# Sums over partitions by way of DRAM instead of products with ones, in a fused state-space and mixture-of-experts kernel

## The chip, the cores and the metric

The kernel runs on one core of a Trainium2 chip. Its time is the device time of one execution in microseconds. Engines are named as the profile names them: PE is TensorE (PEld its weight loads), ACT is ScalarE, DVE is VectorE, POOL is GpSimd, SP is SyncE, which here only issues DMAs.

## The reference

One input sequence of 2048 tokens by 512 channels is normalised, and two layers read the result. Their outputs and the input are added.

```python
x = A_u
xn = _layernorm(x, axis=-1)
return x + _A_ref(xn, ...) + _B_ref(xn, B_w_gate, B_w1, B_w2)

# A: a long convolution of every channel with a generated filter
P = jnp.exp(logdA[:, :, None] * l[None, None, :])
K = jnp.einsum("dn,dnl,dn->dl", Cc, P, dB).real      # filter, 512 x 2048
y = irfft(rfft(pad(xn)) * rfft(pad(K)))[:L] + xn * Dskip

# B: 8 experts, all 8 chosen for every token (K = 8 = E), gates by softmax
for e in range(E):
    h = _silu(xf @ w1[e]) @ w2[e]                    # 512 -> 1792 -> 512
    out = out + w * h
```

All of it is in float32. The kernel gets there with float16 products: every operand is split into a high and a low float16 part, and three products are summed.

## The kernel before, in words

**The main loop.** Eight experts, each over four blocks of 512 tokens (`tb`), each in four steps of hidden columns (`d`, `DQS`: two pairs of columns for d = 0, 1, 2 and one pair for d = 3), each in four slots (`s`). In a slot PE runs one or two groups of the first product (`product`, L1307, into the PSUM tiles `hb`, seven groups for a `d`), then some units of the second product (`pop`, L1290 to L1292, into `y`). ACT copies `hb` on (L1526, L1534, `keep` L1521), applies the activation (L1323) and makes the high part `ahl` (L1327); DVE makes the low part (L1336). A slot of d = 3 has half as many first products as one of d = 0, 1, 2.

**Beside it.** The order on every engine is written out by hand: `slot` is called 510 times, and at its end it does, in this order, some weight steps (`work_on`) and some of the convolution (`bg_run`). Generators hand out the work; `clock` counts the cost given to PE, ACT and DVE; `clock["slot"]` is the number of the slot.

- *Weight steps.* For each next expert the weights are loaded twice. In the first pass ACT squares each piece and sums along the row (`square`, L438). `prepass_end` then adds the partial sums of a row on DVE (L406), adds over the 128 partitions (`pow2_total`), and DVE makes a power of two of the sum, with which ACT and DVE split the weights in the second pass (`w1_split`, `w2_split`, L442 and L445). It runs twice for each expert, once for `w1` and once for `w2`. Between its parts, which are steps of `piece_end`, at least two slots pass.
- *Convolution.* 32 chunks of 16 channels. For a chunk, PE generates the filter (`s4_kernel`, L729). `s4_kernel_out` squares it on ACT with a row sum into `krow` (L737) and copies it to `ksb` (L738). SP stores `ksb` to DRAM as `kd` (L743) and loads it back in another layout as `kt`, in four transfers (L745). `s4_ksplit` adds `krow` over the partitions (`pow2_total`), makes the scale (`s4_kscale`), and splits `kt` (L758 on ACT, L763 on DVE).

**The sum over partitions.** `pow2_total` multiplies the column by a 128 x 128 matrix of ones in float32 (L170), so that every partition gets the sum, in a PSUM bank, and ACT copies it out (L165). There is one such small bank (`ps_s`, tag `s4`), which the filter, the transforms and the transposes use as well: `take_bank` runs the pending read-out before the bank is used again, and `bank_free` says if it may be used in this slot, and runs a pending read-out.

Other names that the prediction needs: the token operand `xop` is reloaded from DRAM by SP in d = 3 (L1517); the partial products `scC` and `scB` are added to by POOL's DMAs (L1492) before ACT reads them.

Of the kernel before, what the change touches and what calls it, by code (L numbers as in the profile page):

```python
# [9 lines left out]
F32 = mybir.dt.float32  # L10
F16 = mybir.dt.float16
I32 = mybir.dt.int32
AF = mybir.ActivationFunctionType
# [4 lines left out]
P = 128  # L18
# [14 lines left out]
def s4_moe_kernel(  # L33
# [15 lines left out]
    nc = tc.nc  # L49
    V, S, T = nc.vector, nc.scalar, nc.tensor  # L50
# [17 lines left out]
    sb = ctx.enter_context(tc.tile_pool(name="sb", bufs=2))  # L68
# [3 lines left out]
    dr = ctx.enter_context(tc.tile_pool(name="dr", bufs=1, space=bass.MemoryType.DRAM))  # L72
# [24 lines left out]
    uts = {}  # L97

    clock = {"slot": 0, "pe": 0.0, "pe0": 0.0, "dve": 0.0, "dve0": 0.0, "left": 0.0,
             "act": 0.0, "act0": 0.0, "pe1": 0.0, "actleft": 0.0}  # L100
    bank = {"out": None, "at": -1}

    def take_bank(out=None):

        f, bank["out"] = bank["out"], None
        if f:
            f()
            bank["at"] = clock["slot"]
        bank["out"] = out

    def bank_free():

        if bank["out"]:
            take_bank()
        return clock["slot"] > bank["at"]

# [44 lines left out]
    def pow2_total(rows, n, nm, out=None):  # L161

        st = sb.tile([P, n], F32, tag="p2a", name=f"st_{nm}", bufs=2)
        def read():
            S.copy(st, tot[:, :n])  # L165
            if out:
                out()
        take_bank(read)
        tot = ps_s.tile([P, 512], F32, tag="s4", name=f"tot_{nm}")
        T.matmul(tot[:, :n], ones, rows, start=True, stop=True)  # L170
        return st

    def pow2_scale(dst, st, nm, add=0):

        it = sb.tile([P, st.shape[-1]], I32, tag="p2b", name=f"it_{nm}", bufs=2)
        V.tensor_scalar(it, st.bitcast(I32), 24, 23, op0=ALU.logical_shift_right, op1=ALU.logical_shift_left)
        V.tensor_scalar(dst.bitcast(I32), it, -1.0, float((204 + add) << 23), op0=ALU.mult, op1=ALU.add)

    def pow2_inverse(dst, src, add=0):

        V.tensor_scalar(dst.bitcast(I32), src.bitcast(I32), -1.0, float((254 + add) << 23), op0=ALU.mult, op1=ALU.add)
# [217 lines left out]
    def w1_scales(sc, st, nm):  # L399
        pow2_scale(sc[:, 0:1], st, nm, -1)  # L400
        pow2_inverse(sc[:, 2:3], sc[:, 0:1], -XSH)
        times(sc[:, 3:4], sc[:, 0:1], 1 - ASH)

    def prepass_end(e, w, n):
        r = sb.tile([P, 1], F32, tag="r2", name=f"r2_{e}_{w}")
        V.tensor_reduce(r, rows[e, w][:, :n], axis=AX.X, op=ALU.add)  # L406
        yield
        st = pow2_total(r, 1, f"w{e}_{w}")
        yield
        if bank["out"]:  # L410
            take_bank()
        if w == 0:
            sc = scales[e] = sb.tile([P, 5], F32, tag="sc", name=f"sc{e}", bufs=2)
            w1_scales(sc, st, f"w{e}")
        else:
            sc = scales[e]
            pow2_scale(sc[:, 1:2], st, f"v{e}")
            pow2_inverse(sc[:, 4:5], sc[:, 1:2])
            V.scalar_tensor_tensor(sc[:, 4:5], sc[:, 4:5], float(2.0 ** (XSH - 1 + ASH)), sc[:, 2:3], op0=ALU.mult, op1=ALU.mult)
            ge_ = sb.tile([P, NT], F32, tag="gse", name=f"gse{e}", bufs=2)  # L420
            gates_e[e] = ge_
            if e > 1:
                V.tensor_scalar(ge_, gate[:, :, e], sc[:, 4:5], None, op0=ALU.mult)
# [17 lines left out]
    def hilo(dst, raw, sc):  # L441
        S.activation(dst[:, 0], raw, AF.Copy, scale=sc)  # L442

        def low():
            V.scalar_tensor_tensor(dst[:, 1], raw, sc, dst[:, 0], op0=ALU.mult, op1=ALU.subtract)  # L445
            clock["dve"] += tt_(raw.free_size())
        return low
# [9 lines left out]

    def w1_split(e, pr, raw):

        dst = w1s[pr].rearrange("p a o c -> p a (o c)")  # L460
        return hilo(dst[:, :, 0:6 * P], raw[:, 0:3, :].rearrange("p o c -> p (o c)"), w1_scale(e, pr))

# [2 lines left out]
        return hilo(dst[:, :, 6 * P:14 * P], tw.rearrange("p o c -> p (o c)"), w1_scale(e, pr))  # L465

    def w2_split(e, pr, raw):
        return hilo(w2s[pr].rearrange("p a f d -> p a (f d)"), raw.rearrange("p a c -> p (a c)"), scales[e][:, 1:2])

    class Item:  # L470
# [6 lines left out]
    done = set()  # L477
# [19 lines left out]
        return it  # L497

    def piece_end(e, w, n, ready):
        st = {}  # L500

        def s0(raw):
            st["g"] = prepass_end(e, w, n)
            step(0)
            clock["dve"] += 0.2

        def step(n):
            st["at"] = now()
            next(st["g"], None)
            done.add((e, w, n))  # L510

        def s1(raw):
            step(1)

        def s2(raw):
            step(2)
            clock["dve"] += 2.5

        def later():
            return now() > st["at"] + 1 and bank_free() and now() + 1 not in turns  # L520
        its = [Item(None, [s0], ready), Item(None, [s1], later), Item(None, [s2], later)]
        for it in its:
            it.e, it.w = e, w
        return its

    def fetch():

# [22 lines left out]
        return True  # L550

    def work_on(limit):
        while limit > 0:
            fetch()
            it = None
            for n, c in enumerate(work[:6]):
                if c.load is None:
                    if n == 0 and can(c):
                        it = c
                        break  # L560
                    if n == 0 and (c.e, c.w, 0) in done:
                        continue
                    break
                if c.raw is not None and can(c):
                    it = c
                    break
            if it is None:
                break
            if it.sums and len(it.steps) == it.n:
                live["tw"], it.at = True, now()  # L570
            low = it.steps.pop(0)(it.raw)
            limit -= 1
            last = not it.steps
            if last:
                work.remove(it)
            if low:
                lows.append((low, last, it.sums and last, it.made))
            elif last and it.load is not None:
                live["n"] -= 1
        fetch()  # L580
# [16 lines left out]
    s4 = {}  # L597
# [136 lines left out]
    def s4_kernel_out(c):  # L734
        ksb = sb.tile([P, 4, 4, NI], F32, tag="ksb", name=f"ksb{c}", bufs=1)
        row = s4["krow", c] = sb.tile([P, 1], F32, tag="krow", name=f"krow{c}", bufs=2)
        S.activation(ksb.rearrange("p j g m -> p (j g m)"), s4["kgen"].rearrange("p g x -> p (g x)"), AF.Square, accum_out=row)  # L737
        S.copy(ksb, s4["kgen"].rearrange("p g (j m) -> p j g m", j=4))  # L738
        clock["act"] += 2 * at_(256)
        s4["ke", c] = now()  # L740
        kt = sb.tile([P, DC, NI], F32, tag="kt", name=f"kt{c}", bufs=1)
        kd = kds[c % 2]
        nc.sync.dma_start(kd, ksb.rearrange("p j g m -> p j (g m)"))  # L743
        for jh in range(4):
            nc.sync.dma_start(kt[32 * jh:32 * jh + 32].rearrange("x (s g) m -> x s (g m)", s=4),  # L745
                              kd[:, jh, :].rearrange("(s x) c -> x s c", s=4))
        s4["kt", c] = kt

    def s4_kscale(c):

# [121 lines left out]
    def at_(n):  # L872

        return n / 1050 + 0.17
# [10 lines left out]
    def now():  # L885
        return clock["slot"]
# [28 lines left out]
    def bank_wait():  # L915
        while not bank_free():
            yield None

    def until(*keys, more=1):

        for key in keys:
            while key not in s4 or now() <= s4[key] + more:
                yield None
# [41 lines left out]
    def s4_ksplit(c):  # L965

        yield from until(("ke", c))
        yield from bank_wait()
        s4["kst", c] = pow2_total(s4["krow", c], 1, f"k{c}", lambda: s4.update({("read", c): now()}))
        s4["total", c] = now()  # L970
        yield None
        while ("read", c) not in s4:
            bank_free()
            if ("read", c) not in s4:
                yield None
        yield from until(("read", c), more=0)
        s4_kscale(c)
        yield 0.6
        yield None
        if c:  # L980
            yield from until(("kf", c - 1), more=0)
        s4_khigh(c)
        yield None
        yield None
        s4_klow(c)
        s4["kl", c] = now()
        yield tt_(256)
# [73 lines left out]
    for pr in range(3, NPR):  # L1061
        for h in range(2):
            n = 2 * (pr - 3) + h
            tag, bufs = ("sE", 1) if n == 0 else ("sCB", 3) if n < 4 else ("stg", 4)
# [303 lines left out]
    turns = set()  # L1368
# [57 lines left out]
    for n, (g, a) in enumerate(halves):  # L1426
        s0 = 20 + 4 * n
# [61 lines left out]
    later = []  # L1489
# [173 lines left out]
```

## Time and profile before

| | |
|---|---|
| time, median of 3 runs (lowest, highest) | 2345.7 us (2345.11, 2345.76) |
| the profiled execution: its own time | 2344.99 us |
| the profiled execution: span of its instructions | 2343.2 us |
| granted PE clock | 1.0 |
| busy: PE, PEld, DVE, ACT, POOL | 2324.7, 1552.8, 1964.2, 1473.5, 339.6 us |
| DMA: share of the 16 engines by SP's queue, by POOL's | 32.4%, 25.3% |

The busy time of an engine is the time in which at least one of its instructions runs, so for PE, whose matmuls overlap, it says that PE is hardly ever without one, and not how fast they follow each other. The span is shorter than the execution's own time by what lies around the instructions (1.8 us). In rows of groups, the numbers behind the bar are the busy time of the group in us, the mean ns of one instruction, and the idle time of the engine just before them with what ended it.

### The profile page before, as it was taken

How to read it: one execution, taken by the hardware profiler on the slowest of the kernel's cores; microseconds unless marked ns; L12 is line 12 of the kernel's file. 1: busy time of each engine (PE TensorE's matmuls, PEld its weight loads, DVE VectorE, ACT ScalarE, POOL GpSimd, SP SyncE). 2: the span in 40 equal slices, each digit the busy share in tenths (PEclk: the TensorE clock that was granted, in tenths of full speed). 3: DMA queues.
4: the chain of work that ended last, by engine and by line, in shares of the span. 5: the costliest groups of instructions: out<-in, count | busy, mean ns of one | idle time of the engine just before them, and what ended most of it. 6: DMA issues, size and time to landing. Idle time of an engine off the chain costs nothing.

```text
span 2343.2 us, 45501 instructions
## 1 busy us (share of the span) xinstructions
PE 2324.7 (99%) x17818; PEld 1552.8 (66%) x17818; DVE 1964.2 (84%) x3814; ACT 1473.5 (63%) x2596; POOL 339.6 (14%) x394
## 2 busy tenths in 40 slices
PE   8999999999999999999999999999999999999999
PEld 4567666666666666666666666666666666666665
DVE  7864878889898899998899989998899988997721
ACT  7586667556665566665666657666576665765543
POOL 0011001121111211101111111111111110111112
PEclk9999999999999999999999999999999999999999
DMA  7586555774667746654556455565465654643456
GB/s 252 167 254 145 144 156 148 163 158 95 139 143 165 155 102 138 154 130 102 115 127 166 120 105 122 132 151 121 103 147 117 150 124 95 150 89 69 83 114 149
DMA packets 330503, 319.68 MB, mean 136 GB/s; under 512 B 190832, under 2 KB 223088, under 8 KB 329968
## 3 DMA queue, kind: packets, MB, share of 16 engines
q1 hardware_dynamic: 274416, 223.17, 32.4%
q0 software_dynamic: 55872, 93.61, 25.3%
q8 instruction: 139, 2.28, 0.4%
q14 instruction: 76, 0.62, 0.1%
HBM read 202.14 MB, written 65.01 MB: 114 GB/s over the span
## 4 chain that ended last, share of the span: by engine, by line
PE 94%; ACT 2%; issue 2%; DVE 1%; DMA 1%; SPq 0%; DVEq 0%; ACTq 0%; POOLq 0%
PE hb L1307 42%; PE y L1291 16%; PE y L1292 16%; PE y L1290 16%; PE kgen L729 1%; PE yp L860 1%; PE kf L800 1%; PE uf L787 1%; DMA scC<-sE 0%; PE tp L274 0%; ACT ahl L1327 0%; ACT fa L1323 0%; ACT w1s L442 0%; PE hb L1572 0%; DMA raw<-in_w_dram 0%
## 5 line engine op out<-in xcount | busy, mean ns | idle before, releaser
L1307 PE MATMUL hb<-xop,w1s 128*128 128x256 f16 x9114 | 1072.8, 273 | 3.3 <-ACT scC L1521 2.0
L1307 PEld LDWEIGHTS <-w1s 128*128 128x128 f16 x9114 | 889.0, 98 | 171.7 <-issue 5.1
L1290 PE MATMUL y<-w2s,ahl 128*128 128x512 f16 x1792 | 679.2, 379 | 0.9 <-ACT ye L1266 0.9
L1292 PE MATMUL y<-w2s,ahl 128*128 128x512 f16 x1792 | 679.2, 379 | 0.0
L1291 PE MATMUL y<-w2s,ahl 128*128 128x512 f16 x1792 | 679.2, 379 | 0.0
L1292 PEld LDWEIGHTS <-ahl 128*128 128x128 f16 x1792 | 175.3, 98 | 211.4
L1492 POOL DMA_DIRECT2D scC<-sE x124 | 117.6, 948 | 1295.0 <-ACT sE L1521 1095.0
L1323 ACT ACTIVATE fa<-hb,sc 128x512 f32<-128x512 f32 (+1 forms) x252 | 160.3, 636 | 199.4 <-PE hb L1307 198.9
L1291 PEld LDWEIGHTS <-ahl 128*128 128x128 f16 x1792 | 175.3, 98 | 162.2 <-issue 1.2
L832 DVE TENSOR_TENSOR s<-s,tm 128x720 f32<-128x720 f32 (+14 forms) x480 | 268.9, 560 | 16.6
L1290 PEld LDWEIGHTS <-ahl 128*128 128x128 f16 x1792 | 175.3, 98 | 161.1
L831 DVE TENSOR_TENSOR tm<-v,k 128x720 f32<-128x720 f32 (+14 forms) x480 | 267.3, 557 | 10.3
L1336 DVE SCALAR_TENSOR_TENSOR ahl<-fa,sc,ahl 128x512 f16<-128x512 f32 (+1 forms) x262 | 178.7, 682 | 57.6 <-ACT ahl L1327 57.3
L1534 ACT COPY hb<-hb 128x512 f32<-128x512 f32 x124 | 64.2, 518 | 240.5 <-PE hb L1307 240.3
L1327 ACT ACTIVATE ahl<-fa,sc 128x512 f16<-128x512 f32 (+1 forms) x262 | 175.8, 671 | 8.5
L1526 ACT COPY hb<-hb 128x512 f32<-128x512 f32 x124 | 64.3, 518 | 176.2 <-PE hb L1307 175.4
L1492 POOL DMA_DIRECT2D scB<-sE x124 | 107.5, 867 | 426.8 <-ACT scB L1521 287.6
L1336 DVE SCALAR_TENSOR_TENSOR ahl<-scB,sc,ahl 128x512 f16<-128x512 f32 x124 | 84.4, 681 | 77.4 <-ACT ahl L1327 74.1
L717 DVE TENSOR_TENSOR tb<-ta,tt 128x64 f32<-128x64 f32 (+2 forms) x192 | 132.0, 687 | 5.7
L711 DVE TENSOR_TENSOR ta<-tb,zr 128x64 f32<-128x64 f32 (+2 forms) x192 | 131.6, 686 | 5.3
L1269 POOL DMA_DIRECT2D oacc<-ye x108 | 95.9, 1339 | 252.8 <-ACT ye L1266 251.1
L714 DVE TENSOR_TENSOR tt<-tb,zi 128x64 f32<-128x64 f32 (+2 forms) x192 | 130.4, 679 | 0.0
(245 smaller groups left out, 2444.6 us busy)
## 6 DMA issues: line engine op xcount, KB each, us to landing
xop<-xd SPq DMA_DIRECT2D x210, 256.0 KB, 4.0
pp<-in_w_dram SPq DMA_DIRECT2D x98, 512.0 KB, 4.2
raw<-in_w_dram SPq DMA_DIRECT2D x56, 512.0 KB, 4.8
oacc<-ye POOLq DMA_DIRECT2D x108, 256.0 KB, 6.2
scC<-sE POOLq DMA_DIRECT2D x93, 256.0 KB, 4.2
scB<-sE POOLq DMA_DIRECT2D x93, 256.0 KB, 3.9
raw<-in_w_dram SPq DMA_DIRECT2D x52, 256.0 KB, 3.4
raw<-in_w_dram SPq DMA_DIRECT2D x104, 128.0 KB, 3.8
```

The source lines that it names most:

```text
L711: V.tensor_tensor(ta, tin, zrv, op=ALU.mult)
L717: V.tensor_tensor(tout, ta, tt, op=ALU.add)
L831: V.tensor_tensor(tm, v3f[:, :, 0:n], kb, op=ALU.mult)
L832: V.tensor_tensor(s3[:, :, m:], s3[:, :, m:], tm, op=ALU.add)
L1290: T.matmul(y, lhs[0], w2s[pr][:, 0, fh, :], start=(c == 0), stop=False)
L1291: T.matmul(y, lhs[0], w2s[pr][:, 1, fh, :], start=False, stop=False)
L1292: T.matmul(y, lhs[1], w2s[pr][:, 0, fh, :], start=False, stop=(c == NF - 1))
L1307: T.matmul(dst[:, q, :], w1s[pr][:, a, wo, k * P:(k + 1) * P], xop[:, xo, b, k, :], start=(first_mm and q == 0 and n == 0), stop=(n == 5), ...
L1323: S.activation(fa, src[:, :n], AF.Silu, scale=w1_unscale(e, d if whole else prs[0]))
L1327: S.activation(ahl[:, 0, :n], fa, AF.Copy, scale=scales[e][:, 3:4])
L1336: V.scalar_tensor_tensor(ahl[:, 1, :n], fa, sc[:, 3:4], ahl[:, 0, :n], op0=ALU.mult, op1=ALU.subtract)
L1492: nc.gpsimd.dma_start(dst, src, accum_op=ALU.add)
```

## The change

For 46 of the 49 sums over partitions (the 32 chunks, and two for each of the experts 1 to 7) the product with ones goes. In its place SP stores the column of 128 numbers to DRAM (`total_send`), loads the 128 numbers back into every partition (`total_fetch`, a broadcast to 128 x 128), and ACT copies that tile onto itself and sums each row (`total_sum`). The three sums of expert 0 stay.

In the convolution, both transfers are issued in `s4_kernel_out`: the store right behind that of `kd`, the load right behind the four of `kt`. The sum comes two slots later, and no longer waits for the small bank. For the weights, the store, the load and the sum are three steps of `piece_end`, which now is one item of five steps instead of three items, and asks for neither the bank nor a free slot of the transposes.

The read-out of the small bank is put off (`bank_free` answers no) in a slot in which `work_on` was allowed two steps and did both. Two assertions check an order and make no instruction.

```diff
     def bank_free():
         if bank["out"]:
+            if clock["two"]:
+                return False
             take_bank()
         return clock["slot"] > bank["at"]
...
+    def total_send(row, nm):
+        rd = dr.tile([P, 1], F32, name=f"rd_{nm}")
+        nc.sync.dma_start(rd, row)
+        return rd
+
+    def total_fetch(rd, nm):
+        bt = sb.tile([P, P], F32, tag="bt", name=f"bt_{nm}", bufs=1)
+        nc.sync.dma_start(bt, rd.rearrange("p a -> (p a)").partition_broadcast(P))
+        return bt
+
+    def total_sum(bt, nm):
+        st = sb.tile([P, 1], F32, tag="p2a", name=f"st_{nm}", bufs=2)
+        S.activation(bt, bt, AF.Copy, accum_out=st)
+        clock["act"] += at_(P) + 0.2
         return st
...
     def prepass_end(e, w, n):
         r = sb.tile([P, 1], F32, tag="r2", name=f"r2_{e}_{w}")
         V.tensor_reduce(r, rows[e, w][:, :n], axis=AX.X, op=ALU.add)
         yield
-        st = pow2_total(r, 1, f"w{e}_{w}")
-        yield
-        if bank["out"]:
-            take_bank()
+        if e:
+            rd = total_send(r, f"w{e}_{w}")
+            yield
+            bt = total_fetch(rd, f"w{e}_{w}")
+            yield
+            st = total_sum(bt, f"w{e}_{w}")
+            yield
+        else:
+            st = pow2_total(r, 1, f"w{e}_{w}")
+            yield
+            if bank["out"]:
+                take_bank()
...
     def piece_end(e, w, n, ready):
...
-        its = [Item(None, [s0], ready), Item(None, [s1], later), Item(None, [s2], later)]
+        it = Item(None, [lambda raw, k=k: step(k) for k in range(5)],
+                  lambda: now() > st["at"] + 1 if "at" in st else ready())
...
     def work_on(limit):
+        clock["two"], n2 = False, limit
         while limit > 0:
...
             limit -= 1
+            clock["two"] = limit == 0 and n2 == 2
...
     def s4_kernel_out(c):
...
         nc.sync.dma_start(kd, ksb.rearrange("p j g m -> p j (g m)"))
+        rd = total_send(row, f"k{c}")
         for jh in range(4):
             nc.sync.dma_start(kt[32 * jh:32 * jh + 32]...)
         s4["kt", c] = kt
+        s4["kbt", c] = total_fetch(rd, f"k{c}")
...
     def s4_ksplit(c):
         yield from until(("ke", c))
-        yield from bank_wait()
-        s4["kst", c] = pow2_total(s4["krow", c], 1, f"k{c}", lambda: s4.update({("read", c): now()}))
-        s4["total", c] = now()
+        s4["kst", c] = total_sum(s4["kbt", c], f"k{c}")
         yield None
-        while ("read", c) not in s4:
-            bank_free()
-            if ("read", c) not in s4:
-                yield None
-        yield from until(("read", c), more=0)
+        yield None
         s4_kscale(c)
```

More of the change, by code (lines that the diff above doesn't have):

```diff
@@ L99, in s4_moe_kernel @@
     clock = {"slot": 0, "pe": 0.0, "pe0": 0.0, "dve": 0.0, "dve0": 0.0, "left": 0.0,
-             "act": 0.0, "act0": 0.0, "pe1": 0.0, "actleft": 0.0}
+             "act": 0.0, "act0": 0.0, "pe1": 0.0, "actleft": 0.0, "two": False}
     bank = {"out": None, "at": -1}
@@ L170, in pow2_total @@
         T.matmul(tot[:, :n], ones, rows, start=True, stop=True)
+        return st
+    def total_send(row, nm):
[10 more added lines that the diff above has]
+        clock["act"] += at_(P) + 0.2
         return st
@@ L458, in w1_split @@
     def w1_split(e, pr, raw):
+        assert e == 0 or (e, 0, 4) in done
         dst = w1s[pr].rearrange("p a o c -> p a (o c)")
@@ L467, in w2_split @@
     def w2_split(e, pr, raw):
+        assert e == 0 or (e, 1, 4) in done
         return hilo(w2s[pr].rearrange("p a f d -> p a (f d)"), raw.rearrange("p a c -> p (a c)"), scales[e][:, 1:2])
@@ L499, in piece_end, with step @@
     def piece_end(e, w, n, ready):
[L500 to L507, printed above, removed]
+        st = {"g": prepass_end(e, w, n)}
+        def step(k):
             st["at"] = now()
             next(st["g"], None)
[L510 to L520, printed above, removed]
-        its = [Item(None, [s0], ready), Item(None, [s1], later), Item(None, [s2], later)]
-        for it in its:
-            it.e, it.w = e, w
-        return its
+            done.add((e, w, k))
+            clock["dve"] += (0.2, 0.0, 0.0, 0.0, 0.9)[k]
+        it = Item(None, [lambda raw, k=k: step(k) for k in range(5)],
+                  lambda: now() > st["at"] + 1 if "at" in st else ready())
+        it.e, it.w = e, w
+        return [it]
     def fetch():
```

## The prediction

> **What bounds the kernel now.** I read the page's busy times and chain first, then the list of who waited for whom on PE.
>
> ```profile
> span 2343.2 us, 45501 instructions
> ...
> PE 2324.7 (99%) x17818; PEld 1552.8 (66%) x17818; DVE 1964.2 (84%) x3814; ACT 1473.5 (63%) x2596; POOL 339.6 (14%) x394
> ...
> PE 94%; ACT 2%; issue 2%; DVE 1%; DMA 1%; SPq 0%; DVEq 0%; ACTq 0%; POOLq 0%
> ```
>
> PE is without a matmul for 2343.2 - 2324.7 = 18.5 us in all, and the chain that ended last is 94% PE. So a change is worth what it takes from PE's stream, less what it adds to PE's waits. The waits are few:
>
> ```profile
> PE tp L308 <- ACT xhl L298: 6.6, 1, 6.6
> PE hb L1307 <- ACT scC L1521: 2.0, 3, 0.9
> PE hb L1105 <- POOL ident masks.py:199: 1.4, 1, 1.4
> PE hb L1307 <- ACT hb L1534: 1.3, 1, 1.3
> PE y L1290 <- ACT ye L1266: 0.9, 1, 0.9
> ```
>
> The first and third are of the start. None is on a DMA, and all that ScalarE costs PE in the main loop is about 5 us.
>
> **What goes from PE.** The changed kernel has the same instructions on PE but for 46 totals, each two passes in the trace (float32); of the 15 `tot_w` one stays.
>
> ```profile
> L170 PEld LDWEIGHTS tot_k<-krow,ones x64: 190/190/190, 331.9 to 2173.5; 128*128 128x128 f32 x64
> L170 PE MATMUL tot_k<-krow,ones x64: 167/208/250, 332.1 to 2173.5; 128*128 128x1 f32 x64
> L170 PE MATMUL tot_w<-r,ones x30: 167/208/250, 34.9 to 1955.4; 128*128 128x1 f32 x30
> ```
>
> Two passes of 208 ns and two loads of 190 ns are not what a total costs, as matmuls overlap. The timeline of PE shows the price, as the distance between starts with a total in between and without:
>
> ```profile
> 326.70 0.38 PE L1292 MATMUL y<-w2s,ahl 128*128 128x512 f16 x1
> 326.91 0.27 PE L1307 MATMUL hb<-xop,w1s 128*128 128x256 f16 x1
> ...
> 331.91 0.38 PE L1292 MATMUL y<-w2s,ahl 128*128 128x512 f16 x1
> 332.12 0.28 PE L170 MATMUL tot_k<-krow,ones 128*128 128x1 f32 x2
> 332.26 0.27 PE L1307 MATMUL hb<-xop,w1s 128*128 128x256 f16 x1
> ```
>
> From the last `y` to the first `hb` it is 0.21 us, and with a total 0.35. A total takes 0.14 us of PE, nothing covers it, and the other totals show the same distance. 46 x 0.14 = **6.4 us less**, 0.27% of the time. That is nearly all that the change can win.
>
> **What else could be won.** The put-off read-out and the other order move ScalarE's work between slots. Up to about 190 us (the 37th slot) all engines keep their order, so of the waits above only the `scC` one at 371 us (0.9) and some tenths later can go: 0 to 1.1 us, and as the same work may bunch elsewhere I take 0.5.
>
> **What ScalarE gets.** For each of 46 sums, a copy of one column (155 ns) becomes a copy of 128 columns with a row sum. Nearest rows:
>
> ```profile
> L165 ACT COPY st_k<-tot_k 128x1 f32<-128x1 f32 x32 | 5.0, 155 | 0.0
> L758 ACT ACTIVATE kh<-kt,ksc 128x256 f16<-128x256 f32 x32 | 16.1, 504 | 0.4 <-DVE ksc L177 0.4
> L737 ACT ACTIVATION_READ_ACCUMULATOR ksb<-kgen 128x1 f32 x32 | 6.4, 199 | 0.0
> ```
>
> 128 columns lie between 155 and 504; I take 0.35 + 0.20 for reading the sum = 0.55 us, 0.4 more than before, 18 us in all on an engine that idles 870. It is a cost only where PE is close behind ScalarE, which the next part prices.
>
> **The new wait.** ScalarE now waits in its own queue for a transfer, and behind it stand the copies of `hb` that PE needs. For a chunk the path after ScalarE's last copy of the filter is: store `kd`, store of the column, wait for `kd`, four issues of `kt`, issue of the broadcast, landing.
>
> ```profile
> 325.66 0.33 SPq L743 DMA_DIRECT2D kd<-ksb  x1
> 327.79 1.75 SPq L745 DMA_DIRECT2D kt<-kd  x4
> ```
>
> ```profile
> kd<-ksb SPq DMA_DIRECT2D x32, 128.0 KB, 3.2
> kt<-kd SPq DMA_DIRECT2D x128, 32.0 KB, 1.9
> ```
>
> The issue of `kt` starts when `kd` has landed. At the medians, 3.2 + 1.75 + 1.9 = 6.9 us; chunk by chunk in the trace the fourth `kt` has landed 4.8 to 13.1 us after the copy, median 7.2. The broadcast is issued right behind it, and I give it `kt`'s landing: 0.5 later, median 7.7. The column's store has no row of its kind (4 bytes from each partition); I take it as hidden behind the four issues, as it is issued 0.4 us after `kd`. The Trainium skill's "DMA: Bandwidth & Descriptors" (Anatomy of one DMA) puts the fixed part of a transfer at about 2.0 us, mostly the receipt of the write; `kd`'s 3.2 us here is above it. By that figure the estimate for the broadcast would be 2.0 + 1.75 + 2.0 = 5.8 us, and with it the waits below would cost PE nothing.
>
> When does ScalarE arrive? The changed kernel's order puts the sum at the end of the second slot after the filter's copy. Taking the slots that it uses from the trace of before, the ends of ScalarE's work two slots apart are 3.2 to 12.6 us apart, ten of 32 below 6.5. A short case (expert 5, d = 3) and a long one (expert 6, d = 0), each by its first and last row:
>
> ```profile
> 1527.26 0.63 ACT L774 CAST uh<-uc 128x256 f16<-128x256 f32 x1
> 1530.79 0.35 ACT L1521 COPY scB<-hb 128x256 f32<-128x256 f32 x1
> ...
> 1969.36 0.51 ACT L1327 ACTIVATE ahl<-scC,sc 128x256 f16<-128x256 f32 x1
> 1981.64 0.59 ACT L1521 COPY sE<-hb 128x512 f32<-128x512 f32 x1 [0.72 <-PE hb L1307]
> ```
>
> That is 3.3 us (1527.89 to 1531.14) and 12.4 (1969.87 to 1982.23). Set against landings of chunks at nearly the same place in a block, ScalarE waits at about 17 of 32 sums, some 42 us together, up to 5 each.
>
> What of this reaches PE? ScalarE already waits that way:
>
> ```profile
> ACT hb L1534 <- PE hb L1307: 240.3, 114, 5.6
> ACT hb L1526 <- PE hb L1307: 175.4, 97, 3.7
> ACT scC L1323 <- DMA scC<-sE: 42.0, 26, 4.4
> ```
>
> 42 us on POOL's transfers in 26 waits, and PE pays next to nothing, since ScalarE mostly stands idle until PE has the next `hb`, about 2 us each time. A tight place is the one after the second slot of d = 3 in expert 7:
>
> ```profile
> 2107.05 0.36 ACT L1521 COPY scC<-hb 128x256 f32<-128x256 f32 x1
> 2108.50 1.47 PE L1307 MATMUL hb<-xop,w1s 128*128 128x256 f16 x12
> ```
>
> The copy ends at 2107.41, PE uses its tile at 2108.50: 1.09 us of room, and a longer delay of ScalarE is a delay of PE. I pushed ScalarE's instructions back in this way at all 46 places, less the idle time they meet, against the next matmul on the tile. A push of 0.4 us costs PE nothing, 1 us at every place 0.5 in sum, 2 us 5.3, 3 us 13.8. The long waits fall into d = 3, where 4 us of push still cost nothing at most places. With the landings above, the sum over the 32 chunks is **1.8 us more** on PE, nearly all from two chunks (expert 7's first, d = 3, and one of expert 6, d = 1). If the broadcast lands 1 us later than taken it is 5, 2 us later 11, 3 us later some 22. The 14 weight sums have a step of two slots for each transfer, so the store is in by the time of the load, and I take 0.
>
> **SP and DVE.** SP gets 92 issues of 0.33 to 0.45 us. For a chunk, the burst behind the filter is 0.8 us longer, and queued behind it are weight loads and, in d = 3, the loads of `xop`. PE waits for no DMA in its list, so I take 0; at most 0.8 for each of the three chunks that fall into the first slot of d = 3, 2.4 us. The store of a weight column makes SP wait for DVE's reduction, issued two slots earlier: 0. DVE's work stays, its order shifts with the chunks, which finish eight slots sooner.
>
> **The sum.** 2344.99 - 6.4 - 0.5 + 1.8 = 2339.9 for the profiled execution, which lies 0.7 below the median of the runs; for the median 2345.7 - 5.1 = **2340.6 us**, -0.22%. What a measurement of this kernel can tell from no change is about 0.2%, 4.7 us, so the line is at 2341.0.
>
> **The rivals.** *The waits eat the gain.* The broadcast lands 0.5 to 2 us later than taken, and PE pays 3 to 11 us instead of 1.8: 2342 to 2350, say **2343**. For it: `kd` alone needs up to 8.5 us when other transfers run, and the forecast is within half a microsecond of the line. Against: the broadcast is small, and the short places have room.
>
> *ScalarE's queue becomes the bound at the sums.* The column's store is the one transfer without a like in the trace. If it lands 2 us or more after the fourth `kt`'s issue, SP stands before the broadcast, the loads behind it stand too, and ScalarE's wait grows everywhere at once. It decides from 2 us of lateness on (then PE pays 11 us and gets 6.9); at 2.5 us PE pays 16, at 3 us 22. With 17, 2345.7 - 6.9 + 17 = **2356**. Against: no landing of a 32 KB transfer in the trace is that late at the median. The skill's page on DMA (Specifications) says that writes under 512 bytes are done as read-modify-write; no run so far shows its price, and it speaks for this rival.
>
> *No change at all* is not to be had from the change not doing what it says: the totals are gone from PE's order.
>
> **How the numbers follow.** The forecast, waits that PE hardly feels, gets 0.42, all of it faster. The first rival gets 0.38 and lies within 0.2%. The second gets 0.20 and is slower. The lower end is all of 6.4 and 1.1 won and nothing paid, 2338. The upper end, 2353, takes in the first rival whole and of the second what lies below its price, and leaves out about 1 in 8 there. The forecast's own range is 2338 to 2341.
>
> **What would show it.** Right: L170 is left with three totals; PE's waits on ScalarE stay below 8 us in sum beyond the start's; ScalarE waits for `bt` at 10 to 20 sums, mostly in d = 3, 30 to 60 us in all; broadcasts land about 2 us after issue. Wrong: PE's list names `hb` behind ScalarE's copies with 10 us or more, or `xop`'s DMA; or SP waits long for `rd` before the broadcast.

## The result, and the profile after

| | before | after |
|---|---|---|
| time, median of 4 runs (lowest, highest) | 2345.73 us (2345.11, 2345.92) | 2529.19 us (2527.45, 2534.57) |
| ratio, 95% interval | | 1.0785 [1.0772, 1.0798] |
| the profiled execution: its own time, span | 2344.99, 2343.2 us | 2528.82, 2527.0 us |
| mean granted PE clock | 1.000 | 0.969 |

The change costs 183 us; 2340.6 us with an upper end of 2353 had been forecast. The page of the changed kernel, the same three rows as before:

```profile
span 2527.0 us, 45454 instructions
...
PE 2369.5 (94%) x17726; PEld 1562.9 (62%) x17726; DVE 1968.6 (78%) x3814; ACT 1483.8 (59%) x2642; POOL 340.3 (13%) x394
...
PE 61%; DMA 17%; issue 9%; ACT 7%; DVE 4%; SPq 1%; POOL 1%; DVEq 0%; POOLq 0%; ACTq 0%
```

PE has 92 matmuls fewer (46 totals of two passes), and yet is busy 44.8 us longer. It is without a matmul for 2527.0 - 2369.5 = 157.5 us, against 18.5 before: 139.0 more. The two make up the 183.8 us by which the span grew. The chain that ended last was 1% DMA and is now 17%. The waits of PE, then of ScalarE, then of SP's queue in the changed kernel (total us, times, longest):

```profile
PE hb L1324 <- ACT hb L1543: 80.8, 16, 10.2
PE hb L1324 <- ACT hb L1551: 32.2, 10, 5.5
PE hb L1324 <- ACT scC L1538: 27.2, 8, 8.6
```

```profile
ACT bt_k L191 <- DMA bt_k<-rd_k: 222.3, 32, 12.7
...
ACT bt_w L191 <- DMA bt_w<-rd_w: 9.8, 4, 5.2
```

```profile
SPq L767 <- DMA kd<-ksb: 147.4, 32, 12.6
...
SPq L185 <- DMA rd_k<-krow: 70.2, 19, 6.3
```

ScalarE waits for the broadcast at all 32 chunks, 222 us together, where 42 us at 17 had been worked out. PE is late behind the three copies that stand behind the sum in ScalarE's queue (L1543, L1551 and `keep` L1538): 140.2 us. SP stands for the column's store before it may issue the broadcast, and waits longer for `kd` than before (105.5 us then, `SPq L745`). One chunk in the timeline of the changed kernel, SP's rows first, then ScalarE's and PE's (start, duration, engine, line, operation; in brackets the idle time before it):

```profile
1091.17 0.32 SPq L764 DMA_DIRECT2D kd<-ksb  x1
1091.54 0.42 SPq L179 DMA_DIRECT2D rd_k<-krow  x1
1092.88 1.82 SPq L767 DMA_DIRECT2D kt<-kd  x4
1099.51 0.34 SPq L185 DMA_DIRECT2D bt_k<-rd_k  x1
...
1105.18 0.31 ACT L191 ACTIVATE bt_k<-bt_k 128x128 f32<-128x128 f32 x1 [9.66 <-DMA bt_k<-rd_k]
1105.40 0.19 ACT L191 ACTIVATION_READ_ACCUMULATOR bt_k<-bt_k 128x1 f32 x1
...
1106.64 4.45 PE L1324 MATMUL hb<-xop,w1s 128*128 128x256 f16 x24 [5.90 <-ACT hb L1543]
```

The issues of `kt` are done by 1094.7 us. Then SP issues nothing for 4.8 us: the store, issued at 1091.54, has not landed. The broadcast goes out at 1099.51 and the sum starts 5.7 us later. Over all 32 chunks, counted from the end of the filter's copy, the medians are: last issue of `kt` done at 8.7 us, broadcast issued at 9.9, sum begun at 15.0. ScalarE arrives at 8.8.

The busy time's growth is a matter of the clock. The same place in windows (busy us of PE, PEld, DVE, ACT and POOL, then the granted PE clock, DMA share and GB/s):

```profile
1097.00:1100.00 3.00, 3.00 (x16) 1.35 (x14) 2.93 (x5) 0.00 (x0) 0.00 (x0) 1.00 0.26 21
1100.00:1106.00 6.00, 0.74 (x7) 0.51 (x6) 0.88 (x1) 0.82 (x3) 0.00 (x0) 0.77 0.44 132
1106.00:1110.00 4.00, 3.36 (x16) 2.37 (x16) 2.33 (x6) 2.53 (x6) 0.00 (x0) 0.50 0.22 86
1110.00:1114.00 4.00, 4.00 (x24) 2.25 (x23) 3.84 (x4) 2.81 (x6) 0.00 (x0) 0.99 0.00 0
```

In the stall the clock falls to a half and is still there for the first 3.4 us of work. The trace has 22 such stretches in the main loop, 147 us together; before there were none. They follow each of the 19 chunks at which PE stood for 3.5 us or longer, and two of the 13 others (stalls of 2.0 and 3.2 us); one comes after another stall, of 3.9 us. The Trainium skill's "TensorE: Matmul & The Clock Gate" (What's actually happening) has half rate after an idle window of about 3.4 us, and full rate again after as long a busy one; this trace agrees for the stalls of 3.5 us or longer, while the two shorter ones lie below that window.

### The profile page after: what moved, and what is told of

The parts are those of the page before. It is cut to its first block, busy times and chain, and to the rows that moved or that the text cites. A ratio compares the mean times of both kernels' runs of the same rounds, so it can differ in the third digit from the quotient of the medians.

```text
span 2527.0 us, 45454 instructions
## 1 busy us (share of the span) xinstructions
PE 2369.5 (94%) x17726; PEld 1562.9 (62%) x17726; DVE 1968.6 (78%) x3814; ACT 1483.8 (59%) x2642; POOL 340.3 (13%) x394
## 4 chain that ended last, share of the span: by engine, by line
PE 61%; DMA 17%; issue 9%; ACT 7%; DVE 4%; SPq 1%; POOL 1%; DVEq 0%; POOLq 0%; ACTq 0%
PE hb L1324 29%; PE y L1307 10%; PE y L1308 10%; PE y L1309 10%; DMA rd_k<-krow 6%; DMA bt_k<-rd_k 5%; DMA kd<-ksb 3%; DMA scC<-sE 2%; ACT ahl L1344 1%; DVE tm L854 1%; PE kgen L750 1%; DVE s L855 1%; SPq L767 1%; DVE ahl L1353 1%; ACT fa L1340 1%
## 5 line engine op out<-in xcount | busy, mean ns | idle before, releaser
L1324 PE MATMUL hb<-xop,w1s 128*128 128x256 f16 x9114 | 1112.0, 279 | 140.4 <-ACT hb L1543 80.8
L1324 PEld LDWEIGHTS <-w1s 128*128 128x128 f16 x9114 | 906.8, 100 | 344.7 <-issue 141.0
L1551 ACT COPY hb<-hb 128x512 f32<-128x512 f32 x124 | 64.3, 518 | 209.0 <-PE hb L1324 208.9
L1353 DVE SCALAR_TENSOR_TENSOR ahl<-scC,sc,ahl 128x512 f16<-128x512 f32 x124 | 84.4, 681 | 127.3 <-ACT ahl L1344 123.2
L1543 ACT COPY hb<-hb 128x512 f32<-128x512 f32 x124 | 64.5, 520 | 159.3 <-PE hb L1324 159.1
L191 ACT ACTIVATE bt_k<-bt_k 128x128 f32<-128x128 f32 x32 | 9.9, 309 | 222.3 <-DMA bt_k<-rd_k 222.3
```

The costliest lines, as they stand in the source:

```text
L1324: T.matmul(dst[:, q, :], w1s[pr][:, a, wo, k * P:(k + 1) * P], xop[:, xo, b, k, :], start=(first_mm and q == 0 and n == 0), stop=(n == 5), ...
L1353: V.scalar_tensor_tensor(ahl[:, 1, :n], fa, sc[:, 3:4], ahl[:, 0, :n], op0=ALU.mult, op1=ALU.subtract)
```

## The experiments

Each time is the median, with the ratio to the kernel before on the same chip and its interval. Where there is no ratio, the kernel ran once. In the runs with 4-byte stores the trace tells the landing of only some transfers, and the medians of landings there stand on 3 to 15 of them. The theories: the trip's latency holds ScalarE's queue, and PE behind it (the second rival, larger); or the transfers disturb others; or the new order does the harm.

### The chunks alone, the weights alone

```diff
-        if e:
-            rd = total_send(r, f"w{e}_{w}")
...
+        st = pow2_total(r, 1, f"w{e}_{w}")
```

> Only the 32 chunk sums go by way of DRAM; the 14 weight sums use the product with ones as before. Theory (ScalarE waits in its own queue for the chunks' broadcasts, PE then waits for the copies of hb behind it, and PE's clock is halved for some us after each such stall): nearly all of the 183 us stays, 2505 to 2530 us, ScalarE waits about 220 us for bt_k. Rival A (every trip of 128 four-byte pieces slows the other transfers, so the loss goes with the number of trips): 32/46 of it, about 2470 us.

2543.67 us, above the 2505 to 2530 that I expected and 14 us above the changed kernel; why it is above that, this single run does not show. ScalarE waits for `bt_k` at all 32 chunks:

```profile
ACT bt_k L191 <- DMA bt_k<-rd_k: 227.1, 32, 13.8
```

The chunks are the whole loss.

```diff
-        rd = total_send(row, f"k{c}")
...
-        s4["kbt", c] = total_fetch(rd, f"k{c}")
...
-        s4["kst", c] = total_sum(s4["kbt", c], f"k{c}")
+        s4["kst", c] = pow2_total(s4["krow", c], 1, f"k{c}", lambda: s4.update({("read", c): now()}))
```

> Only the 14 weight sums go by way of DRAM; the 32 chunk sums use the product with ones as before. Theory: the weight sums have two slots for each transfer, ScalarE waits for them only some 10 us in all, and 14 totals give PE 2 us back: 2342 to 2350 us. Rival A (loss by the number of trips): 14/46 of 183, about 2400 us.

2345.53 us, 1.000 [0.999, 1.001]. ScalarE's waits for the sums, and the row of the store:

```profile
ACT bt_w L191 <- DMA bt_w<-rd_w: 11.2, 4, 5.7
```

```profile
rd_w<-r SPq DMA_DIRECT2D x14, 0.5 KB, 8.4
```

With two slots for each transfer the same trip costs nothing that shows, though its store takes 8.4 us in the median (of the six landings that the trace tells). The 14 x 0.14 = 2.0 us that PE should gain lie within the interval.

### No transfers at all

```diff
-        nc.sync.dma_start(rd, row)
...
-        nc.sync.dma_start(bt, rd.rearrange("p a -> (p a)").partition_broadcast(P))
...
-        S.activation(bt, bt, AF.Copy, accum_out=st)
+        S.activation(bt, ones, AF.Copy, accum_out=st)
```

> As changed, but both transfers are left out: ScalarE sums a constant tile of the same size in the same place, so the scales are not those of the data. Theory and rivals A and B: the whole loss is gone and 46 totals of 0.14 us are won, 2337 to 2342 us. Rival C (the new order and the put-off read-out, or the longer ScalarE instruction, cost PE by themselves): over 2350 us.

2340.66 us, 0.9977 [0.9968, 0.9987]. Its page, PE's largest waits on ScalarE in the main loop, and two waits that later runs are set against:

```profile
span 2339.0 us, 45351 instructions
...
PE 2319.5 (99%) x17726; PEld 1542.5 (66%) x17726; DVE 1963.2 (84%) x3814; ACT 1483.7 (63%) x2642; POOL 340.5 (15%) x394
```

```profile
PE hb L1321 <- ACT hb L1548: 1.3, 1, 1.3
PE hb L1321 <- ACT scC L1535: 1.2, 3, 0.9
```

```profile
SPq L764 <- DMA kd<-ksb: 95.5, 32, 8.7
```

```profile
ACT scC L1337 <- DMA scC<-sE: 35.2, 27, 4.8
```

The order of the changed kernel, its ScalarE work and its shorter PE stream are all here, and 5.2 us are won against the kernel before on the same chip. So neither the order nor ScalarE's longer sum does harm; the transfers do. PE has the same 17726 matmuls as in the changed kernel and is busy 2319.5 instead of 2369.5 us: 50 us are the clock's.

### ScalarE held, without transfers

```diff
-        S.activation(bt, bt, AF.Copy, accum_out=st)
+        for _ in range(14 if nm[0] == "k" else 1):
+            S.activation(bt, ones, AF.Copy, accum_out=st)
```

> As the run without the trip, but at each of the 32 chunk sums ScalarE does the constant sum 14 times, some 6.5 us, with no transfer at all. Theory (a push of ScalarE is all it takes): PE pays about 65 to 80 us by pushing the trace of before, and its clock is halved for some us after stalls, a third on top: 2420 to 2450 us, granted clock below 0.99. Rival F (the clock and the stalls come from the transfers): under 2360 us, clock 1.0.

2444.1 us, at a mean clock of 0.988.

```profile
PE hb L1322 <- ACT hb L1541: 43.8, 19, 4.9
PE hb L1322 <- ACT hb L1549: 16.4, 9, 4.3
PE hb L1322 <- ACT scC L1536: 14.6, 9, 4.9
```

ScalarE's busy time is 162 us above the kernel without transfers, 5.1 us at each of the 32 sums, and this alone costs 103 us, behind the same three copies and with the same fall of the clock. This shows the mechanism without a DMA. The changed kernel's waits are 6.9 us in the mean and up to 12.7, and cost 188 us.

### The sum later

```diff
-        bt = sb.tile([P, P], F32, tag="bt", name=f"bt_{nm}", bufs=1)
+        bt = ones if nm[0] == "k" else sb.tile([P, P], F32, tag="bt", name=f"bt_{nm}", bufs=1)
...
-        yield from until(("ke", c))
+        yield from until(("ke", c), more=3)
```

> As changed, but the sum of a chunk comes four slots after the filter's copy instead of two; both transfers are issued where they were, so SP is held by the column's store just as long. Theory: ScalarE arrives some 9 us later, at about 18 us, and the broadcast is in at about 15: waits remain in the short blocks alone, 2338 to 2365 us. Rival B (SP's queue, held by the store's landing, delays the loads behind it, and that is what costs): the loss stays, over 2480 us.

2380.47 us, 1.0147 [1.0132, 1.0162], above the 2338 to 2365 that I expected. The chunks' broadcast goes into a tile of its own here (`ones`). Rows of its transfers (KB, median us from issue to landing) and of the waits of SP and PE:

```profile
ones<-rd_k SPq DMA_DIRECT2D x32, 64.0 KB, 4.6
...
rd_k<-krow SPq DMA_DIRECT2D x32, 0.5 KB, 8.9
```

```profile
SPq L767 <- DMA kd<-ksb: 185.0, 32, 11.4
...
SPq L185 <- DMA rd_k<-krow: 56.0, 14, 6.3
```

```profile
PE hb L1324 <- DMA xop<-xd: 19.3, 6, 5.5
```

149 us come back when ScalarE no longer waits. What is left, 40 us above the kernel without transfers, is another thing: the store takes 8.9 us, SP waits 185.0 us for `kd` (95.5 without transfers), and PE now waits for `xop`, which SP issues behind them. Then the broadcast was moved as well:

```diff
-                  lambda: now() > st["at"] + 1 if "at" in st else ready())
+                  lambda: now() > st["at"] + (0, 0, 1, 2, 1)[len(it.steps)] if "at" in st else ready())
...
-        s4["kbt", c] = total_fetch(rd, f"k{c}")
+        s4["krd", c] = rd
...
-        yield from until(("ke", c))
-        s4["kst", c] = total_sum(s4["kbt", c], f"k{c}")
+        yield from until(("ke", c), more=2)
+        bt = total_fetch(s4["krd", c], f"k{c}")
+        yield from until(("ke", c), more=4)
+        s4["kst", c] = total_sum(bt, f"k{c}")
```

> As changed, but the broadcast of a chunk is issued three slots after the filter's copy and its sum comes five slots after it; the weights' broadcast is issued a slot later after its store. Theory (ScalarE's wait, and beside it SP held by the store's landing, which was the rest in the run with only the sum later): both go, and 46 totals of 0.14 us are won: 2338 to 2345 us. Rival B (many small pieces slow the other transfers, wherever the waits are): 2360 us or more.

2372.39 us, 1.0114 [1.0099, 1.0129], a miss: with store and broadcast both given time I expected 2338 to 2345 us. SP's and ScalarE's waits:

```profile
SPq L767 <- DMA kd<-ksb: 174.1, 32, 10.8
...
SPq L185 <- DMA rd_k<-krow: 22.0, 5, 5.9
```

```profile
ACT scC L1340 <- DMA scC<-sE: 69.0, 34, 6.4
```

SP's wait for the store fell from 56.0 to 22.0 us, but its wait for `kd` stayed at 174.1 us and ScalarE's for POOL's `scC` is 69.0, against 95.5 and 35.2 without transfers. This points at a harm to transfers that nobody queued behind the 4-byte store; the next runs test it.

### Store or broadcast, one at a time

Only the stores, read by nobody (the kernel without transfers, with the stores put back):

```diff
+        nc.sync.dma_start(rd, row)
```

> As the run without the trip, but the column of 128 numbers is stored to DRAM as in the change; nothing reads it, and nobody waits for it but the queue's own reuse. The sums are of a constant tile. Theory G (the pieces of four bytes also delay other transfers in flight): SP's waits for kd rise from 95 us to 140 or more, ScalarE's for scC above 45 us, 2345 to 2370 us. Rival H (only the store's own landing is late): 2338 to 2343 us, waits as without the trip.

2360.14 us, 1.0058 [1.0043, 1.0073]. Waits of SP, ScalarE and PE:

```profile
SPq L766 <- DMA kd<-ksb: 179.6, 32, 12.2
```

```profile
ACT scC L1339 <- DMA scC<-sE: 107.0, 42, 7.9
```

```profile
PE hb L1323 <- DMA xop<-xd: 9.2, 9, 3.3
```

Nothing reads these stores, and yet `kd`, which was issued ahead of them, makes SP wait 179.6 us where the kernel without transfers has 95.5, and `scC` makes ScalarE wait 107.0 us (35.2 there). SP also stands 14.5 us at five places until a store has landed, before it issues a later load, mostly `xop`. The cost of all this is 19.5 us.

The same with 64 bytes from each partition in place of 4:

```diff
-        rd = dr.tile([P, 1], F32, name=f"rd_{nm}")
-        nc.sync.dma_start(rd, row)
+        rd = dr.tile([P, 16], F32, name=f"rd_{nm}")
+        nc.sync.dma_start(rd, ones[:, 0:16])
```

> As the run with the store alone, but 64 bytes from each partition. Theory G with a limit between 64 and 512 bytes: SP's waits for kd as with the store of four bytes, the same time within 5 us. Theory G with the four bytes as such the cause: waits for kd near 95 us, 2338 to 2345 us.

2340.92 us.

```profile
rd_k<-ones SPq DMA_DIRECT2D x32, 8.0 KB, 2.2
```

```profile
SPq L766 <- DMA kd<-ksb: 71.0, 32, 7.8
```

Sixteen times the bytes land in 2.2 us and harm nothing that shows. As many pieces go out. What differs is their size, how close they lie in DRAM (128 pieces in 512 bytes, against 8 KB), and the tile that they come from (a constant one here).

Only the broadcast, of a row that is in DRAM from the start:

```diff
-        nc.sync.dma_start(bt, rd.rearrange("p a -> (p a)").partition_broadcast(P))
+        nc.sync.dma_start(bt, rd[0:1, :].rearrange("p a -> (p a)").partition_broadcast(P))
```

> As changed, but without the stores: the broadcast reads a row that was stored once at the start, and is issued in its place behind kt; the scales are not those of the data. Theory G: the broadcast is issued when kt is and is in 2 to 5 us later, at 8 to 11 us; ScalarE waits 40 to 80 us for it, 2341 to 2358 us. Rival D (the broadcast is late by itself whatever the store does): waits of 150 us and more, over 2420 us.

2364.94 us, 1.0088 [1.0071, 1.0105], somewhat above what I expected.

```profile
ACT bt_k L191 <- DMA bt_k<-cst: 69.3, 19, 7.8
```

Then the whole path with a store of 512 bytes from each partition (a constant tile), one row of which is broadcast:

```diff
-        rd = dr.tile([P, 1], F32, name=f"rd_{nm}")
-        nc.sync.dma_start(rd, row)
+        rd = dr.tile([P, P], F32, name=f"rd_{nm}")
+        nc.sync.dma_start(rd, ones)
...
-        nc.sync.dma_start(bt, rd.rearrange("p a -> (p a)").partition_broadcast(P))
+        nc.sync.dma_start(bt, rd[0:1, :].rearrange("p a -> (p a)").partition_broadcast(P))
```

> As changed, but the store to DRAM writes 512 bytes from each partition (a constant tile) instead of 4, and the broadcast reads one row of it; the scales are not those of the data. Theory (the store of 4 bytes from each partition is late by itself, some 8 us, and holds the issue of the broadcast): the broadcast is in at about 10 us after the filter's copy instead of 15, 2345 to 2375 us. Rival D (the broadcast, 128 reads of one row, is the late one): ScalarE's waits stay near 220 us, over 2450 us.

2361.09 us, 1.0064 [1.0049, 1.0079].

```profile
rd_k<-ones SPq DMA_DIRECT2D x32, 64.0 KB, 2.9
bt_k<-rd_k SPq DMA_DIRECT2D x32, 64.0 KB, 3.9
```

With a store that lands in 2.9 us the whole path costs no more than the broadcast alone.

In place of the broadcast, a plain load of the whole stored tile:

```diff
+        nc.sync.dma_start(bt, rd)
```

> As the run with the wide store, but the load reads back 512 different bytes for each partition instead of one row for all. Theory (both transfers of the prediction's kind, as kd and kt): the tile is in at about 8 us, 2340 to 2350 us, as forecast. Rival D: a large step below the wide store's time; rival E (any load behind kt is late, because SP's queue is): the same time as with the wide store.

2348.3 us, 1.0009 [0.9999, 1.0018]. Its page, its transfers, and the waits of ScalarE and PE:

```profile
span 2346.9 us, 45445 instructions
...
PE 2321.9 (99%) x17726; PEld 1540.8 (66%) x17726; DVE 1962.5 (84%) x3814; ACT 1482.9 (63%) x2642; POOL 339.4 (14%) x394
```

```profile
rd_k<-ones SPq DMA_DIRECT2D x32, 64.0 KB, 2.9
bt_k<-rd_k SPq DMA_DIRECT2D x32, 64.0 KB, 1.9
```

```profile
ACT bt_k L191 <- DMA bt_k<-rd_k: 41.4, 16, 6.7
```

```profile
PE hb L1324 <- ACT hb L1543: 4.6, 2, 4.2
```

This is the trip as the prediction took it: nothing slow ahead of the broadcast, and a landing of 1.9 us. ScalarE waits 41.4 us at 16 sums (42 at 17 had been worked out).

By itself the store costs 19.5 us and the broadcast 24.3 above the kernel without transfers; together, in the changed kernel, 188. The two delays add on one path, ahead of a wait whose price rises faster than its length.

### A version that keeps the trip

From these runs: send few, longer pieces, give each transfer its own slots, and leave the weights as they were. DVE transposes the column in blocks of 32, so that four partitions hold 128 bytes each, and the store has four pieces.

```diff
+        V.transpose(btk[:, 0:32], btk[:, 32:64])
+        rd = dr.tile([4, 32], F32, name=f"rd_{nm}")
+        nc.sync.dma_start(rd, btk[::32, 0:32])
...
+        yield from until(("ke", c), more=0)
+        rd = total_send(btk, f"k{c}")
+        yield from until(("ke", c), more=2)
+        bt = total_fetch(rd, f"k{c}")
+        yield from until(("ke", c), more=4)
+        s4["kst", c] = total_sum(bt, f"k{c}")
```

> Chunk sums alone by way of DRAM (weights by the product with ones), but DVE first turns the column, in blocks of 32, into four rows of 128 bytes, so the store has four pieces instead of 128 of four bytes; store, broadcast and sum are one, three and five slots after the filter's copy. Theory G (the 128 pieces of four bytes are late and hold up other transfers): without them nothing waits, 32 totals of 0.14 us are won: 2339 to 2345 us. Rival I (a trip through DRAM on SP's queue costs whatever its pieces): 2355 us or more, as in the run with both transfers later.

2343.19 us, 0.9989 [0.9980, 0.9999]: faster than before by 2.4 us, though hardly beyond what this measurement tells.

```profile
ACT btk L194 <- DMA btk<-rd_k: 15.0, 5, 4.6
```

```profile
SPq L188 <- DMA rd_k<-btk: 22.6, 13, 2.6
```

32 of the 46 totals are off PE here. No transfer at all gives 2340.66 us, so 2.5 us more is all that a better trip could win, and 2.0 of them would be the 14 weight totals. The run changes the pieces, the slots and the weights at once; slots alone, with 4-byte pieces, gave 2372.39 us.

## Why the prediction was wrong, point by point

**PE's stream: right.** The kernel without transfers is 5.2 us below before, and its interval of 3.0 to 7.5 us holds the 6.4 + 0.5. The re-ordering's 0.5 can't be told apart from it.

**ScalarE's sum: right.** In the timeline above the copy and the reading of its sum end 0.41 us after its start (0.55 taken), and without transfers it costs nothing that shows.

**The step that failed: the landing of the broadcast.** It had two assumptions, both without a row of their kind. *"The column's store ... hidden behind the four issues"*: it lands in about 8.9 us, not within the two or so that the issues cover. It holds SP up to 6.3 us at 19 chunks, and it also slows `kd`, which the sum had at 3.2 us; that is why the last `kt` is issued at 8.7 us in the median and not at 3.2 + 1.75 = 4.95. *"I give it `kt`'s landing"*: a chunk's broadcast takes 3.9 to 5.4 us in the experiments, about 5 from issue to sum in the changed kernel, and not 1.9. The sum can start at 15.0 us instead of 7.7.

**The price of a wait: too low, even where the landing is as taken.** The wide store with the plain load has the waits that were worked out, and costs 7.6 us above the kernel without transfers where 1.8 had been taken: PE stands 5.5 us longer (25.0 against 19.5) and is busy 2.4 us longer (2321.9 against 2319.5). The largest single stall, 4.2 us, is at one of the two places named, in expert 6 (d = 1, at 1940.9 us); at the other, expert 7's first chunk, PE doesn't stand for as much as 0.9 us. So with both assumptions true, the time would have been that of the first rival's span (2342 to 2350).

**What no step had: the clock.** Pushing instructions through the trace counts stalls, not what follows them. 50 us of the changed kernel are PE at a lower clock.

**SP: the 0 was wrong in kind.** Only the time of the issues had been counted. With the stores alone PE waits 9.2 us for `xop`, with the sum later 19.3. In the changed kernel PE has no wait for `xop` in its list; ScalarE's lateness comes first.

**The weights' sums at 0: right**, by the run with them alone.

**The rivals.** "ScalarE's queue becomes the bound at the sums" is what happened, with the chain that it named: SP stands before the broadcast, and ScalarE's wait grows everywhere at once. It was priced for 2.5 to 3 us of lateness and got 0.20. The sum starts 7.3 us late (15.0 against 7.7), some 2.7 times as much, and costs eleven times as much (188 us against 17). The steps of the push (0.5, 5.3, 13.8 us for 1, 2, 3) had shown such a curve; the range should have followed it to the slowest transfers that the trace of before had, and a store of an unseen kind should not have been bounded by its neighbours' medians. The rule cited for this rival, that writes below 512 bytes are done as read-modify-write (the Trainium skill, "DMA: Bandwidth & Descriptors", Specifications), spoke for the right side, but its border isn't what decides here: 64 bytes are below it too and land in 2.2 us. The fixed part of about 2.0 us on the same page of the Trainium skill (Anatomy of one DMA) agrees with the 64-byte store and with the plain load, and not with the 4-byte store. The Trainium skill gives it there for transfers that GpSimd issues; these are issued by SP.

## What to carry to other kernels

A transfer that an in-order engine waits for is priced with everything queued behind that engine, and the price isn't linear: ask what a delay three times as long would cost before a chance is given to it. Where the trace has no transfer of the kind (piece size, broadcast), measure it alone or give it several slots; here the trip of the 14 weight sums, with slots between its parts, cost nothing that showed, and that of the 32 chunks, without them, 188 us. Slots don't help against a transfer that slows the others: before a column goes to DRAM, turn it into a few rows.

## What was not expected of the hardware

- A store of 4 bytes from each of 128 partitions lands in 8.4 to 9.6 us; of 64 bytes, in 2.2; of 512 bytes, in 2.9 (medians, the last two for the chunks). While it is under way, other transfers are slower too: SP's wait for `kd` goes from 95.5 to 179.6 us over 32 chunks. The trace with the stores alone narrows down where the time goes: at the 14 chunks where SP's queue has nothing else under way, its last packet is recorded 2.8 us after the store's issue in the median (at most 3.9), and the store lands 8.4 us after it (at least 7.6). What is long is the time from the packets to the landing. Why stays open: no run has 4-byte pieces that lie far apart in DRAM, so their size and their closeness can't be told apart.
- A broadcast of one row of 512 bytes to 128 partitions takes 3.9 us where a plain load of as many bytes takes 1.9, at the chunks. At the 14 weight sums of the same two runs it is 4.1 against 3.9, so the difference depends on what goes on beside it. Why stays open as well.
- PE's granted clock fell to a half at every one of the 19 chunks whose stall was 3.5 us or longer; the 22 stretches at half clock cost the changed kernel 50 us of PE's busy time.
